# Sparse attention and a channel MLP in one kernel: masks of the later batches written into PSUM by ScalarE, one wide product with U for each batch, and the first scores of a batch two slots later

## The chip, the core and the metric

The kernel runs on one core of one Trainium2 chip. The metric is the device time of one execution in microseconds (us). The engines named below are PE (TensorE, matrix products), DVE (VectorE), ACT (ScalarE), POOL (GpSimd) and SP (SyncE, which issues most DMAs). Each engine carries out its own instructions strictly in the order in which they were written into its stream; engines wait for each other through semaphores.

## The reference

Attention with two kinds of heads, and then a token mixer of low rank and a channel MLP. Heads 0 to 3 see a window of 32 positions (local heads); heads 4 to 7 see positions with the same remainder by 32 (strided heads).

```python
B, H, S, D = 8, 8, 576, 64
scores = q @ k.T / sqrt(D)                      # for each batch and head
mask_local   = (rel >= 0) & (rel < 32)          # heads 0-3, rel = row - column
mask_strided = (rel >= 0) & (same remainder by 32)  # heads 4-7
scores = where(mask, scores, -1e9)
attn = exp(scores - max); attn = attn / (sum(attn) + 1e-9)
x = (attn @ v) as (8, 576, 512)                 # heads side by side
u = x + (x.T @ U @ V).T                         # U: 576x32, V: 32x576
out = u + relu(u @ w_ch1) @ w_ch2               # 512 -> 2048 -> 512
```

## The kernel before

**GEMM stages.** The MLP is done in nine stages, n = 0 to 8, of 512 rows each: stage n is batch n's rows 0 to 511, and stage 8 holds the 64 last rows of all eight batches. A stage has 16 steps, fc = 0 to 15, one for each 128 hidden channels. `gemm1(fc)` makes 12 matmuls of 128x512 into a PSUM tile `ph` (three products for precision, with `uh`, `ul` the high and low part of u, and a high and a low part of the weights). ScalarE takes the relu of it into `gh` (line 652), VectorE makes the low part `gl` (line 653). `gemm2(fc)` makes 12 matmuls from `gh` and `gl` into the two tiles `acc` (line 665); it stands one step behind `gemm1`, so a step is 24 matmuls. At a stage's end `finish` (line 672, four VectorE additions) takes `acc` out, and `split` makes the next stage's `uh` (ScalarE, line 639, four casts) and `ul` (VectorE, line 640, four subtractions) from `raw`.

**Attention between the matmuls.** While stage n runs, batch n+1's attention and mixing are issued in 32 slots, two to a step. `advance(slot)` spreads a fixed number of pieces (the yields of the generator `attention`) evenly between a first and a last slot; `A_EARLY` holds first slot, last slot and number of pieces for stage 0, `A_LATE` for stages 1 to 6. Batches 0 and 1 have their attention before the first stage. For a later batch the order is:

- `local_pairs`: two pairs of local heads. The mask is put into the PSUM tile `px` by two matmuls (line 340), 36 pairs of small score matmuls add to it (line 346), VectorE takes maximum and difference (lines 356, 357), ScalarE the exponential (361), PE transposes (368), ScalarE copies (371), PE multiplies by v (381), VectorE normalises (390 to 397). `px` is a single buffer of two banks.
- `mix_t`, half 0: x^T U for the 256 columns of the local heads (matmuls of lines 514 and 518, then `ta`, lines 523 and 525, and `tst`, lines 527 to 529).
- `strided_copies` (ScalarE, lines 487 and 491), then `mix_t`, half 1, for the columns of the strided heads, `mix_u` (product with V, line 537, and addition, line 539), `mix_tail` (line 546, addition line 552), `transposes` (line 619) and DMAs into `raw`.

**Strided heads.** They use no matmul: `strided_heads` makes products on GpSimd and sums them on VectorE, on a schedule of its own (`S0`, `S1`). Scores come first (GpSimd line 442, VectorE reductions line 444, 27 a batch); the softmax (lines 453 to 461) falls at the boundary of two stages; the second half, with v (GpSimd line 470, VectorE reductions line 472, 27 a batch, whose input grows from 128x64 to 128x576 elements over the first nine), fills the first part of the next stage.

In stage 0, VectorE and ScalarE also convert the last weights from 64-bit words (`weights`, lines 131, 132 and 206).

A scheduler fixes each engine's stream; `tc.issue_after(x)` forces what is issued inside it to stand behind instruction x.

Of the kernel before, what the change touches and what calls it, by code (L numbers as in the profile page):

```python
# [7 lines left out]
F32 = mybir.dt.float32  # L8
F32R = mybir.dt.float32r
# [4 lines left out]
ALU = mybir.AluOpType  # L14
# [1 line left out]
NEG = -1.0e9  # L16
ATT_BUFS = 5
NSP = 2
N_EARLY = 20
N_LATE = 48  # L20
N_STRIDED = 66
LAG = 1
CLA = 4
# [1 line left out]
N_LEAD = 4  # L25
BEHIND = 5
A_EARLY = (5, 28, N_EARLY)
A_LATE = (1, 28, N_LATE)
A_TAIL = (4, 20, 8)
S0 = {2: 16, **{b: 32 * (b - 1) - 12 for b in range(3, 8)}}  # L30
S1 = (14, 14)
# [6 lines left out]
def fused_kernel(ctx, tc, pairs, strided, U, V, w_in, masks, eye, out):  # L38
    nc = tc.nc
    B, S, DM = out.shape  # L40
    D = 64
# [10 lines left out]
    ap_ = ctx.enter_context(tc.tile_pool(name="ap", bufs=1))  # L52
# [28 lines left out]
    marks = {}  # L81
# [24 lines left out]
    mask_l, ident_b = masks_sb[:, 0:320], masks_sb[:, 320:448]  # L106
    U_sb = const.tile([128, 5, R], F32, name="U_sb")
# [8 lines left out]
    raws, w_parts = {}, {}  # L116
# [101 lines left out]
    xgs, tails, tsts, o_str = {}, {}, {}, {}  # L218
    halves = [slice(64 * hh, 64 * hh + 64) for hh in range(2)]
# [109 lines left out]
        for i4 in range(2):  # L329
            far_dma(out=xt[tb + 32 * i4:tb + 32 * i4 + 32, 256:512], in_=ov[16 + i4])  # L330

    def scores(kT, qT, mask):

        sp = psx2()
        done = marks.setdefault("scores", [])
        with tc.issue_after(done[-1]) if len(done) == 1 else nullcontext():
            for n in range(WARM.get(len(done), 0)):
                nc.tensor.matmul(sp[:, 0, :], zeros[:, 0:128], zeros[:, 128:640], start=True, stop=True, skip_group_check=True)
        for hh in range(2):
            nc.tensor.matmul(sp[:, hh, 0:320], ident_b, mask, start=True, stop=False, skip_group_check=True)  # L340
        for c in range(NCH):
            t, c4 = c // 4, c % 4
            k0 = max(0, 32 * c - 32)
            x0 = 64 * t + (0 if c else 32)
            for hh, rows in enumerate(halves):
                last = nc.tensor.matmul(sp[32 * c4:32 * c4 + 32, hh, x0:64 * t + 64], qT[rows, 32 * c:32 * c + 32],  # L346
                                        kT[rows, k0:32 * c + 32], start=False, stop=True, skip_group_check=True,
                                        tile_position=(64 * hh, 32 * c4))
        done.append(last.ins)
        return sp[:, :, 0:320].rearrange("p h (t x) -> p h t x", x=64)  # L350
# [22 lines left out]

    def outputs(PT, vt):

        op = psx2()
        for c in range(NCH):
            t, c4 = c // 4, c % 4
            for o4 in (c4,) if t < 4 else (c4, c4 + 2):
                for hh, rows in enumerate(halves):  # L380
                    last = nc.tensor.matmul(op[32 * o4:32 * o4 + 32, hh, (D + 1) * t:(D + 1) * t + D + 1],  # L381
                                            PT[rows, 32 * c:32 * c + 32], vt[rows, c], start=True, stop=True,
                                            skip_group_check=True, tile_position=(64 * hh, 32 * o4))
        marks.setdefault("PV", []).append(last.ins)
        return op[:, :, 0:5 * (D + 1)].rearrange("p h (t x) -> p h t x", x=D + 1)

# [14 lines left out]
    def local_pairs(b):  # L401

        xg, xt = x_tiles(b)
        tb = 64 * (b % 2)
        for pr in range(2):
            kT, qT = load_qk(b, pr)
            vt = load_v(b, pr)
            for _ in range(2):
                yield
            sp = scores(kT, qT, mask_l)  # L410
            yield
            s_sb = yield from probabilities(sp)
# [83 lines left out]
    def x_tiles(b):  # L496
        if b not in xgs:
            xgs[b] = xp.tile([128, 4, DM], F32, name="xg")
        if b // 2 not in tails:
            tails[b // 2] = xp.tile([128, DM], F32, name="xt")  # L500
        return xgs[b], tails[b // 2]

    def mix_t(b, half):

        xg, xt = x_tiles(b)
        tb = 64 * (b % 2)
        cs = slice(256 * half, 256 * half + 256)
        ps_a = psx1()[:, 0:256]
        if b not in tsts:
            tsts[b] = ap_.tile([96, DM], F32R, name="tst")  # L510
        tst = tsts[b]
        with tc.issue_after(marks["acc"][2 + half]) if b < NSP else nullcontext():
            for j in range(4):
                nc.tensor.matmul(ps_a[32 * j:32 * j + 32, :], U_sb[:, j, :], xg[:, j, cs], start=True, stop=False,  # L514
                                 skip_group_check=True, tile_position=(0, 32 * j))
        for j in range(4):
            part = slice(64 * j, 64 * j + 64)
            nc.tensor.matmul(ps_a[32 * j:32 * j + 32, part], U_sb[tb:tb + 64, 4, :],
                             xt[tb:tb + 64, 256 * half + 64 * j:256 * half + 64 * j + 64], start=False, stop=True,
                             skip_group_check=True, tile_position=(tb, 32 * j))  # L520
        yield
        ta = att([32, 256], "ta")
        nc.scalar.copy(out=ta, in_=ps_a[0:32, :])  # L523
        for j in range(1, 4):
            nc.vector.tensor_tensor(out=ta, in0=ps_a[32 * j:32 * j + 32, :], in1=ta, op=ALU.add)  # L525
        yield
        nc.scalar.copy(out=tst[0:32, cs], in_=ta)
        nc.scalar.copy(out=tst[64:96, cs], in_=ta)
        nc.vector.tensor_tensor(out=tst[32:64, cs], in0=ta, in1=tst[0:32, cs].bitcast(F32), op=ALU.subtract)
        yield  # L530

    def mix_u(b):
# [62 lines left out]
    def attention(b):  # L595
        if b >= NSP:
            yield from local_pairs(b)
            yield from mix_t(b, 0)
            yield "strided"
            yield from strided_copies(b)  # L600
            yield from mix_t(b, 1)
            yield
            yield from mix_u(b)
            yield from mix_tail(b)
            yield from transposes(b)
        else:
            yield from mix_tail(0)
            for half in range(2):
                yield from mix_t(b, half)
            yield from mix_u(b)  # L610
            yield from mix_tail(b)
            yield from transposes(b)
# [31 lines left out]
    def gemm1(fc, dcs=range(NDC)):  # L644
        ph = ps_h.tile([128, 512], F32, name="ph")
        for dc in dcs:
            for i, (part, ut) in enumerate(((0, uh), (0, ul), (1, uh))):
                nc.tensor.matmul(ph, w_parts[fc, 0][:, part, 128 * dc:128 * dc + 128], ut[:, dc, :],  # L648
                                 start=(dc == dcs[0] and i == 0), stop=(dc == dcs[-1] and i == 2))
# [3 lines left out]
        low = nc.vector.scalar_tensor_tensor(out=gl, in0=ph, scalar=0.0, in1=gh.bitcast(F32), op0=ALU.max, op1=ALU.subtract)  # L653
        marks.setdefault("gl", []).append(low.ins)
        return gh, gl
# [172 lines left out]
```

## Time and profile before

| | before |
|---|---|
| median of 3 runs | 930.89 us (1476.99, 928.80, 930.89) |
| profiled execution, its own time | 928.37 us |
| its span in the trace | 926.1 us |
| mean granted TensorE clock | 0.991 |
| PE busy | 902.6 us (97% of the span) |
| DVE busy | 548.6 us (59%) |
| POOL busy | 338.4 us (37%) |
| ACT busy | 244.2 us (26%) |

All durations below are of that one profiled execution. The span is the time from its first to its last instruction; 2.3 us of the execution lie outside it. An engine's busy time counts its arithmetic, not the instructions that only wait or issue DMAs. The granted clock is the share of the full TensorE clock that the chip's throttle allowed. A bracket at the end of a row gives the idle time of the engine ahead of it, and which instruction's end released it.

### The profile page before, as it was taken

To read this page: it belongs to the slowest core of one execution; us is meant where nothing else is said; L and a number is where in the kernel's file an instruction comes from. 1 tells how busy PE (TensorE), PEld (TensorE's weight loads), DVE (VectorE), ACT (ScalarE), POOL (GpSimd) and SP (SyncE) were. 2 spreads that over 40 slices of the span, in tenths; PEclk is the share of its full clock that TensorE was granted. 3 is DMA by queue.
4 is the path that set the end of the run, shared out by engine and by line. 5 is a ranking of instruction groups with operands and counts; after the bars stand their busy time and mean duration, and the time that the engine had idled before them with its cause. 6 is when DMAs were issued, how large, how long until landed. Compare 5 with 4: busy or idle time off the path is not lost.

```text
span 926.1 us, 16819 instructions
## 1 busy us (share of the span) xinstructions
PE 902.6 (97%) x6997; PEld 718.0 (78%) x6998; DVE 548.6 (59%) x895; ACT 244.2 (26%) x478; POOL 338.4 (37%) x378
## 2 busy tenths in 40 slices
PE   7899989999999999999999999999999999999997
PEld 4667767777887788778877787778877888888885
DVE  4579996665886588658765786667863341122111
ACT  3457522142123312331224121422142111121110
POOL 1223493343853393429433764356530000000000
PEclk9899999999999999999999999999999999999999
DMA  9869313201230125011500141014200230001001
GB/s 352 299 205 357 117 54 107 73 2 52 76 145 2 52 55 178 1 52 33 181 8 18 50 168 50 1 53 148 73 1 1 57 120 17 1 1 46 0 1 46
DMA packets 39036, 75.29 MB, mean 81 GB/s; under 512 B 6464, under 2 KB 22864, under 8 KB 37040
## 3 DMA queue, kind: packets, MB, share of 16 engines
q1 hardware_dynamic: 27312, 66.87, 20.7%
q10 hardware_dynamic: 10560, 4.73, 2.0%
q0 software_dynamic: 1088, 2.62, 0.8%
q8 instruction: 55, 0.90, 0.4%
q14 instruction: 21, 0.17, 0.1%
HBM read 54.14 MB, written 11.67 MB: 71 GB/s over the span
## 4 chain that ended last, share of the span: by engine, by line
PE 84%; DVE 4%; DMA 2%; POOL 1%; issue 1%; ACT 0%; SPq 0%; DVEq 0%; ACTq 0%; POOLq 0%
PE acc L665 40%; PE ph L648 39%; PE px L381 1%; DMA w<-in_w_dram 1%; PE px L346 1%; DVE cv L132 1%; DVE s_st L444 1%; PE px L368 1%; PE px L514 1%; DMA od<-x 1%; PE px L537 1%; DMA st<-in_strided_dram 1%; DVE w L206 1%; POOL tmp L442 1%; DVE gl L653 0%
## 5 line engine op out<-in xcount | busy, mean ns | idle before, releaser
L653 DVE SCALAR_TENSOR_TENSOR gl<-ph,gh 128x512 fp32r<-128x512 f32 x144 | 98.9, 688 | 230.1 <-ACT gh L652 229.4
L648 PE MATMUL ph<-uh,w 128*128 128x512 f32 x648 | 215.9, 394 | 0.0
L652 ACT ACTIVATE gh<-ph 128x512 fp32r<-128x512 f32 x144 | 86.2, 599 | 476.9 <-PE ph L648 400.8
L470 POOL TENSOR_TENSOR tmp<-st,s_st 128x448 f32<-128x448 f32 (+7 forms) x162 | 137.3, 876 | 190.8 <-DVE st L472 106.8
L442 POOL TENSOR_TENSOR tmp<-st 128x576 f32<-128x576 f32 (+6 forms) x162 | 175.0, 1121 | 76.5 <-DMA st<-in_strided_dram 66.6
L665 PE MATMUL acc<-w,gh 128*128 128x512 f32 x648 | 196.8, 391 | 0.0
L648 PEld LDWEIGHTS ph<-uh,w 128*128 128x128 f32 x648 | 121.9, 189 | 26.8
L665 PEld LDWEIGHTS acc<-w,gh 128*128 128x128 f32 x648 | 121.3, 188 | 25.6
L472 DVE TENSOR_REDUCE st<-tmp 128x64 f32<-128x64 f32 (+8 forms) x162 | 136.3, 878 | 7.8 <-POOL tmp L470 7.0
L648 PE MATMUL ph<-ul,w 128*128 128x512 f32 x324 | 126.8, 391 | 0.0
L665 PE MATMUL acc<-w,gl 128*128 128x512 f32 x324 | 121.6, 392 | 4.1 <-DVE gl L653 4.1
L444 DVE TENSOR_REDUCE s_st<-tmp 128x9 f32<-128x576 f32 (+6 forms) x162 | 87.2, 563 | 17.5 <-POOL tmp L442 16.7
L665 PEld LDWEIGHTS acc<-w,gl 128*128 128x128 f32 x324 | 61.0, 188 | 18.4 <-DVE gl L653 5.2
L648 PEld LDWEIGHTS ph<-ul,w 128*128 128x128 f32 x324 | 61.1, 189 | 12.6
L487 ACT COPY xg<-st 32x256 f32<-32x256 f32 x96 | 38.8, 404 | 9.1 <-DVE st L472 7.7
L525 DVE TENSOR_TENSOR ta<-px,ta 32x256 f32<-32x256 f32 x42 | 17.6, 420 | 36.5 <-ACT ta L523 35.6
L672 DVE TENSOR_TENSOR xg<-acc,xg 128x512 f32<-128x512 f32 x36 | 22.9, 682 | 13.4 <-PE acc L665 13.4
L539 DVE TENSOR_TENSOR xg<-px,xg 128x512 f32<-128x512 f32 x28 | 18.0, 684 | 11.9 <-PE px L537 11.9
L648 PE MATMUL ph<-uh,w6a 128*128 128x512 f32 x72 | 24.3, 398 | 0.0
L640 DVE TENSOR_TENSOR ul<-raw,uh 128x512 fp32r<-128x512 f32 x32 | 21.1, 682 | 5.3 <-ACT uh L639 5.3
L648 PE MATMUL ph<-uh,w1a 128*128 128x512 f32 x72 | 23.9, 391 | 0.0
L648 PE MATMUL ph<-uh,w2a 128*128 128x512 f32 x72 | 23.9, 391 | 0.0
(265 smaller groups left out, 1252.9 us busy)
## 6 DMA issues: line engine op xcount, KB each, us to landing
w<-in_w_dram SPq DMA_DIRECT2D x9, 1024.0 KB, 13.3
out_dram<-xg SPq DMA_DIRECT2D x32, 256.0 KB, 2.1
v<-in_pairs_dram SPq DMA_DIRECT2D x12, 585.0 KB, 5.1
st<-in_strided_dram SPq DMA_DIRECT2D x6, 1152.0 KB, 5.4
qk<-in_pairs_dram SPq DMA_DIRECT2D x12, 576.0 KB, 5.1
late<-in_pairs_dram SPq DMA_DIRECT2D x8, 585.0 KB, 8.3
late<-in_pairs_dram SPq DMA_DIRECT2D x8, 576.0 KB, 8.1
raw<-bt SPq DMA_DIRECT2D x128, 32.0 KB, 1.9
```

The costliest lines, as they stand in the source:

```text
L442: nc.gpsimd.tensor_tensor(out=tmp[:, 0:n], in0=sk[:, j0:j0 + n], in1=sq[:, i:i + 1].broadcast_to([128, n, D]), op=ALU.mult)
L444: late.append(lambda tmp=tmp, n=n, i=i, j0=j0: nc.vector.tensor_reduce(out=s_st[:, i, j0:j0 + n], in_=tmp[:, 0:n], axis=AX.X, op=ALU.add))
L470: nc.gpsimd.tensor_tensor(out=tv, in0=sv[:, 0:i + 1, d0:d0 + step], in1=s_st[:, i, 0:i + 1].broadcast_to([128, i + 1, step]), op=ALU.mult)
L472: late.append(lambda tv=tv, i=i, d0=d0, step=step: nc.vector.tensor_reduce(out=o_st[:, i, d0:d0 + step], in_=tv.rearrange("p j d -> p d j" ...
L487: nc.scalar.copy(out=xg[32 * i4:32 * i4 + 32, :, cs], in_=o_st[rows, i4:16:4, :])
L539: nc.vector.tensor_tensor(out=xg[:, t + s, :], in0=pv[:, s, :], in1=xg[:, t + s, :], op=ALU.add)
L640: nc.vector.tensor_tensor(out=lo, in0=raw[:, :, :, dc, :], in1=hi.bitcast(F32), op=ALU.subtract)
L648: nc.tensor.matmul(ph, w_parts[fc, 0][:, part, 128 * dc:128 * dc + 128], ut[:, dc, :], start=(dc == dcs[0] and i == 0), stop=(dc == dcs[-1 ...
L652: marks.setdefault("gh", []).append(nc.scalar.activation(out=gh, in_=ph, func=AF.Relu).ins)
L653: low = nc.vector.scalar_tensor_tensor(out=gl, in0=ph, scalar=0.0, in1=gh.bitcast(F32), op0=ALU.max, op1=ALU.subtract)
L665: last = nc.tensor.matmul(accs[n][s // 2][:, s % 2, :], gt[:, cs], w_parts[fc, 1][:, part, :], start=(fc == 0 and i == 0 and n > 0), stop= ...
L672: nc.vector.tensor_tensor(out=ot, in0=accs[n][s // 2][:, s % 2, :], in1=ot, op=ALU.add)
```

## The change

Batches 2 to 7 (the third to the eighth) are changed in these places; batches 0 and 1 keep their masks on PE:

- The mask of a pair of local heads is written into `px` by one ScalarE copy that broadcasts it to both banks (`masked`), a piece of its own ahead of the scores. The scores may be issued only behind the last matmul of the newest `gemm1`.
- In `outputs`, only the matmuls of the first of five column blocks carry `start`; the others are issued behind those. (This holds for all batches.)
- `mix_t` is one group of 512 columns, after the strided copies, for stage 0's batch 1 too.
- `A_LATE` starts at slot 3 and not 1; the numbers of pieces are 47 and 17, and not 48 and 20.

```diff
-A_LATE = (1, 28, N_LATE)          # N_LATE = 48, N_EARLY = 20
+A_LATE = (3, 28, N_LATE)          # N_LATE = 47, N_EARLY = 17
...
+    def masked():
+        sp = psx2()
+        nc.scalar.copy(out=sp[:, :, 0:320], in_=mask_l.broadcast_to([128, 320, 2]).rearrange("p x h -> p h x"))
+        return sp
...
     def outputs(PT, vt):
         op = psx2()
+        first = None
         for c in range(NCH):
             t, c4 = c // 4, c % 4
-            for o4 in (c4,) if t < 4 else (c4, c4 + 2):
-                for hh, rows in enumerate(halves):
-                    last = nc.tensor.matmul(op[...], PT[...], vt[...], start=True, stop=True, ...)
+            with tc.issue_after(first) if t else nullcontext():
+                for o4 in (c4,) if t < 4 else (c4, c4 + 2):
+                    for hh, rows in enumerate(halves):
+                        last = nc.tensor.matmul(op[...], PT[...], vt[...], start=t == 0, stop=True, ...)
+            if t == 0:
+                first = last.ins
...
     def local_pairs(b):
-            sp = scores(kT, qT, mask_l)
+            sp = masked()
+            yield
+            with tc.issue_after(marks["ph"][-1]):
+                sp = scores(kT, qT, mask_l, sp)
...
-    def mix_t(b, half):
-        cs = slice(256 * half, 256 * half + 256)
-        ps_a = psx1()[:, 0:256]
+    def mix_t(b):
+        ps_a = psx1()
         for j in range(4):
-                nc.tensor.matmul(ps_a[32 * j:32 * j + 32, :], U_sb[:, j, :], xg[:, j, cs], ...)
+                nc.tensor.matmul(ps_a[32 * j:32 * j + 32, :], U_sb[:, j, :], xg[:, j, :], ...)
         for j in range(4):
-            part = slice(64 * j, 64 * j + 64)
+            part = slice(128 * j, 128 * j + 128)
...
-        ta = att([32, 256], "ta")
+        ta = att([32, 512], "ta")
...
     def attention(b):
             yield from local_pairs(b)
-            yield from mix_t(b, 0)
             yield "strided"
             yield from strided_copies(b)
-            yield from mix_t(b, 1)
+            yield from mix_t(b)
...
     def gemm1(fc, dcs=range(NDC)):
-                nc.tensor.matmul(ph, w_parts[fc, 0][...], ut[:, dc, :], ...)
+                last = nc.tensor.matmul(ph, w_parts[fc, 0][...], ut[:, dc, :], ...)
+        marks.setdefault("ph", []).append(last.ins)
```

Line numbers grow with the change: 444 becomes 465, 472 becomes 493 (reductions of the strided heads), 552 becomes 569 (addition of the tail), 619 becomes 634 (transposes), 640 becomes 655 (`ul`), 653 becomes 669 (`gl`), 672 becomes 688 (`finish`); on PE, 665 becomes 681 (`gemm2`) and 546 becomes 563 (the tail's product).

The change also moves instructions in the streams of the engines. VectorE at the boundary of stages 3 and 4, from `gl` of the last steps of stage 3 (first row) to `gl` of fc 0 of stage 4 (last row), before:

```order
L653 SCALAR_TENSOR_TENSOR gl<-ph,gh 128x512 x2
L458 TENSOR_REDUCE m_st<-s_st 128x18
L640 TENSOR_TENSOR ul<-raw,uh 128x512
L459 TENSOR_SCALAR m_st<-m_st 128x18
L640 TENSOR_TENSOR ul<-raw,uh 128x512 x2
L460 RECIPROCAL m_st<-m_st 128x18
L640 TENSOR_TENSOR ul<-raw,uh 128x512
L461 TENSOR_TENSOR s_st<-s_st,m_st 128x324
L472 TENSOR_REDUCE st<-tmp 128x64 x5
L672 TENSOR_TENSOR xg<-acc,xg 128x512 x2
L472 TENSOR_REDUCE st<-tmp 128x64
L672 TENSOR_TENSOR xg<-acc,xg 128x512 x2
L653 SCALAR_TENSOR_TENSOR gl<-ph,gh 128x512 x2
```

The same place with the change:

```order
L655 TENSOR_TENSOR ul<-raw,uh 128x512
L481 RECIPROCAL m_st<-m_st 128x18
L655 TENSOR_TENSOR ul<-raw,uh 128x512
L482 TENSOR_TENSOR s_st<-s_st,m_st 128x324
L655 TENSOR_TENSOR ul<-raw,uh 128x512 x2
L493 TENSOR_REDUCE st<-tmp 128x64 x5
L688 TENSOR_TENSOR xg<-acc,xg 128x512 x2
L493 TENSOR_REDUCE st<-tmp 128x64 x2
L688 TENSOR_TENSOR xg<-acc,xg 128x512 x2
L493 TENSOR_REDUCE st<-tmp 128x64 x2
L669 SCALAR_TENSOR_TENSOR gl<-ph,gh 128x512
L493 TENSOR_REDUCE st<-tmp 128x32 x2
```

Six reductions of the strided heads stood ahead of the `gl` of fc 0; now nine do. At the boundary of stages 1 and 2 it is ten, at that of 4 and 5 eleven, and at both the second pair of `finish` stands behind ten of them.

ScalarE at the same boundary, from the last two relus of stage 3, with the change (`s_st` is the exponential of the strided softmax):

```order
L668 ACTIVATE gh<-ph 128x512 x2
L476 ACTIVATE s_st<-s_st 128x324
L343 CAST px<-masks_sb 128x2x320
L654 CAST uh<-raw 128x512 x4
L668 ACTIVATE gh<-ph 128x512 x3
```

The new copy of the mask for the first pair of the next batch (line 343) stands ahead of the four casts of `uh`; before, the casts followed line 455, the same exponential, directly.

VectorE in stage 3 ahead of `gl` of fc 13 (the last row), before; `px` in line 552 is the tail's product:

```order
L444 TENSOR_REDUCE s_st<-tmp 128x6
L552 TENSOR_TENSOR xt<-px,xt 64x512
L444 TENSOR_REDUCE s_st<-tmp 128x9
L444 TENSOR_REDUCE s_st<-tmp 128x7
L653 SCALAR_TENSOR_TENSOR gl<-ph,gh 128x512
```

PE at the tail's product (line 546), before; `w_1500` holds the weights of fc 12, `w_1544` those of fc 13:

```order
L648 MATMUL ph<-uh,w_1544 128x512
L665 MATMUL acc<-w_1500,gh 128x512 x4
L546 MATMUL px<-tst,Vst 64x512
L665 MATMUL acc<-w_1500,gl 128x512
L665 MATMUL acc<-w_1500,gh 128x512 x2
```

With the change VectorE still has two reductions, of widths 7 and 9, between the tail's addition (now line 569) and `gl` (now 669). On PE the tail's product has moved; `w_1531` now holds the weights of fc 13, `w_1572` those of fc 14:

```order
L663 MATMUL ph<-uh,w_1572 128x512
L563 MATMUL px<-tst,Vst 64x512
L681 MATMUL acc<-w_1531,gh 128x512 x4
L681 MATMUL acc<-w_1531,gl 128x512
L681 MATMUL acc<-w_1531,gh 128x512 x2
```

It stood inside `gemm2` of fc 12 and stands 20 matmuls later, directly ahead of `gemm2` of fc 13, whose fifth matmul reads the `gl` of fc 13. So VectorE's addition of the tail, which has to have that product, and the `gl` of fc 13 behind it, now follow a matmul that comes four matmuls ahead of the first user of this `gl`.

Scores of a stage's two pairs stand at 2.5 and 6.0 steps into the stage (before: 1.0 and 4.3), the product with U at 10.0 steps (before: 7.7 and 9.5). At fc 0 of a stage, `gemm2` now has four matmuls with `gh` ahead of the first with `gl` (before: two), and the third writes the second tile of `acc`.

More of the change, by code (lines that the diff above doesn't have):

```diff
@@ L18 @@
 NSP = 2
-N_EARLY = 20
-N_LATE = 48
+N_EARLY = 17
+N_LATE = 47
 N_STRIDED = 66
@@ L330, in od_reads, with with_mask @@
             far_dma(out=xt[tb + 32 * i4:tb + 32 * i4 + 32, 256:512], in_=ov[16 + i4])
-    def scores(kT, qT, mask):
-        sp = psx2()
+    def with_mask(sp, mask):
         done = marks.setdefault("scores", [])
@@ L340, in scores @@
             nc.tensor.matmul(sp[:, hh, 0:320], ident_b, mask, start=True, stop=False, skip_group_check=True)
+    def masked():
+        sp = psx2()
+        nc.scalar.copy(out=sp[:, :, 0:320], in_=mask_l.broadcast_to([128, 320, 2]).rearrange("p x h -> p h x"))
+        return sp
+    def scores(kT, qT, mask, sp=None):
+        if sp is None:
+            sp = psx2()
+            with_mask(sp, mask)
+        done = marks.setdefault("scores", [])
         for c in range(NCH):
@@ L376, in outputs @@
         op = psx2()
+        first = None
         for c in range(NCH):
             t, c4 = c // 4, c % 4
-            for o4 in (c4,) if t < 4 else (c4, c4 + 2):
-                for hh, rows in enumerate(halves):
-                    last = nc.tensor.matmul(op[32 * o4:32 * o4 + 32, hh, (D + 1) * t:(D + 1) * t + D + 1],
-                                            PT[rows, 32 * c:32 * c + 32], vt[rows, c], start=True, stop=True,
-                                            skip_group_check=True, tile_position=(64 * hh, 32 * o4))
+            with tc.issue_after(first) if t else nullcontext():
+                for o4 in (c4,) if t < 4 else (c4, c4 + 2):
+                    for hh, rows in enumerate(halves):
+                        last = nc.tensor.matmul(op[32 * o4:32 * o4 + 32, hh, (D + 1) * t:(D + 1) * t + D + 1],
+                                                PT[rows, 32 * c:32 * c + 32], vt[rows, c], start=t == 0, stop=True,
+                                                skip_group_check=True, tile_position=(64 * hh, 32 * o4))
+            if t == 0:
+                first = last.ins
         marks.setdefault("PV", []).append(last.ins)
@@ L501, in x_tiles @@
         return xgs[b], tails[b // 2]
-    def mix_t(b, half):
+    def mix_t(b):
         xg, xt = x_tiles(b)
         tb = 64 * (b % 2)
-        cs = slice(256 * half, 256 * half + 256)
-        ps_a = psx1()[:, 0:256]
[L509 to L512, printed above, removed]
+        ps_a = psx1()
+        tst = tsts[b] = ap_.tile([96, DM], F32R, name="tst")
+        with tc.issue_after(marks["acc"][3]) if b < NSP else nullcontext():
             for j in range(4):
-                nc.tensor.matmul(ps_a[32 * j:32 * j + 32, :], U_sb[:, j, :], xg[:, j, cs], start=True, stop=False,
+                nc.tensor.matmul(ps_a[32 * j:32 * j + 32, :], U_sb[:, j, :], xg[:, j, :], start=True, stop=False,
                                  skip_group_check=True, tile_position=(0, 32 * j))
         for j in range(4):
-            part = slice(64 * j, 64 * j + 64)
-            nc.tensor.matmul(ps_a[32 * j:32 * j + 32, part], U_sb[tb:tb + 64, 4, :],
-                             xt[tb:tb + 64, 256 * half + 64 * j:256 * half + 64 * j + 64], start=False, stop=True,
-                             skip_group_check=True, tile_position=(tb, 32 * j))
+            part = slice(128 * j, 128 * j + 128)
+            nc.tensor.matmul(ps_a[32 * j:32 * j + 32, part], U_sb[tb:tb + 64, 4, :], xt[tb:tb + 64, part],
+                             start=False, stop=True, skip_group_check=True, tile_position=(tb, 32 * j))
         yield
-        ta = att([32, 256], "ta")
+        ta = att([32, 512], "ta")
         nc.scalar.copy(out=ta, in_=ps_a[0:32, :])
@@ L526, in mix_t @@
         yield
-        nc.scalar.copy(out=tst[0:32, cs], in_=ta)
-        nc.scalar.copy(out=tst[64:96, cs], in_=ta)
-        nc.vector.tensor_tensor(out=tst[32:64, cs], in0=ta, in1=tst[0:32, cs].bitcast(F32), op=ALU.subtract)
+        nc.scalar.copy(out=tst[0:32], in_=ta)
+        nc.scalar.copy(out=tst[64:96], in_=ta)
+        nc.vector.tensor_tensor(out=tst[32:64], in0=ta, in1=tst[0:32].bitcast(F32), op=ALU.subtract)
         yield
@@ L607, in attention @@
             yield from mix_tail(0)
-            for half in range(2):
-                yield from mix_t(b, half)
+            yield from mix_t(b)
             yield from mix_u(b)
@@ L647, in gemm1 @@
             for i, (part, ut) in enumerate(((0, uh), (0, ul), (1, uh))):
-                nc.tensor.matmul(ph, w_parts[fc, 0][:, part, 128 * dc:128 * dc + 128], ut[:, dc, :],
-                                 start=(dc == dcs[0] and i == 0), stop=(dc == dcs[-1] and i == 2))
+                last = nc.tensor.matmul(ph, w_parts[fc, 0][:, part, 128 * dc:128 * dc + 128], ut[:, dc, :],
+                                        start=(dc == dcs[0] and i == 0), stop=(dc == dcs[-1] and i == 2))
+        marks.setdefault("ph", []).append(last.ins)
         gh = mp.tile([128, 512], F32R, name="gh", bufs=2)
```

## Prediction

> **What bounds the kernel now.** The page's chain of the work that ended last comes first, then the table of stretches, cut at the stages.
>
> ```profile
> PE 84%; DVE 4%; DMA 2%; POOL 1%; issue 1%; ACT 0%; SPq 0%; DVEq 0%; ACTq 0%; POOLq 0%
> ...
> 362.90:460.30 97.40, 97.40 (x743) 77.77 (x740) 68.08 (x114) 25.45 (x55) 51.03 (x55) 1.00 0.20 64
> ...
> 365.90 2.72 PE ph L648 x12
> ```
>
> The chain is PE's. In stage 3 (the second row: length, busy time of PE, weight loads, DVE, ACT and POOL, then the clock) PE has no idle time in 97.4 us. Twelve GEMM matmuls take 2.72 us, 0.227 each; 16 steps of 24 make 87.0 us, and the other 10.4 are attention's small matmuls. DVE has 68 us of work, so it bounds nothing by its sum, but its order does as soon as something PE needs stands late in it. So I count what PE loses in matmuls, then ask of each `gl`, the only thing that PE needs from DVE in every step, whether it still comes in time.
>
> **The change: what goes.** The masks first, from PE's timeline around the first and the second scores of stage 3's start (first piece) and 21 us later:
>
> ```profile
> 361.71 0.39 PE L648 MATMUL ph<-uh,w1a 128*128 128x512 f32 x1
> 362.03 0.92 PE L346 MATMUL px<-qk 64*32 64x32 f32 x72
> 362.88 0.73 PE L665 MATMUL acc<-w0b,gh 128*128 128x512 f32 x2
> ...
> 382.77 0.39 PE L665 MATMUL acc<-w3b,gh 128*128 128x512 f32 x1
> 383.00 0.45 PE L340 MATMUL px<-masks_sb 128*128 128x320 bf16 x2
> 383.38 0.92 PE L346 MATMUL px<-qk 64*32 64x32 f32 x72
> 384.23 0.50 PE L665 MATMUL acc<-w3b,gh 128*128 128x512 f32 x1
> ...
> 404.80 0.39 PE L648 MATMUL ph<-ul,w 128*128 128x512 f32 x1
> 405.11 0.64 PE L514 MATMUL px<-xg,U_sb 128*32 128x256 f32 x8
> 405.68 0.32 PE L518 MATMUL px<-xt,U_sb 64*32 64x64 f32 x8
> 405.93 0.50 PE L648 MATMUL ph<-uh,w 128*128 128x512 f32 x1
> ```
>
> Scores alone cost 362.88 - 361.71 - 0.23 = 0.94; with masks 384.23 - 382.77 - 0.23 = 1.23. So a mask pair costs 0.29, and 11 of the 12 pairs save 3.2 (the first one, below, stands in an idle time). Half a product with U costs 405.93 - 404.80 - 0.23 = 0.90, two 1.80. For one group of twice the width the trace has no row; it costs between 1.0 (a matmul's length does not grow) and 1.8 (it doubles). I take 1.44, since 0.90 is mostly a fixed part: a saving of 0.36, times 6 batches 2.2 (0 to 4.8). Batch 2's scores, scattered in five pieces over stages 0 and 1 now, become one group; each piece costs some 0.1 extra to enter and leave: 0.5.
>
> Stage 0 is bound by DVE until 139 us, and there the order changes:
>
> ```profile
> 130.39 0.50 PE L665 MATMUL acc<-w,gl 128*128 128x512 f32 x1 [1.90 <-DVE gl L653]
> ...
> 137.59 0.45 PE L340 MATMUL px<-masks_sb 128*128 128x320 bf16 x2
> 139.35 0.50 PE L665 MATMUL acc<-w,gl 128*128 128x512 f32 x1 [1.32 <-DVE gl L653]
> ...
> 136.13 2.45 DVE L132 SCALAR_TENSOR_TENSOR cv<-w,cv 128x1024 int32<-128x1024 int32 x1
> ...
> 140.33 1.29 DVE L619 STREAM_TRANSPOSE bt<-xg 128x512 f32<-128x512 f32 x2
> ...
> 130.00:132.00 2.00, 1.61 (x7) 1.31 (x8) 2.00 (x4) 0.71 (x2) 2.00 (x2) 0.96 0.12 33
> 132.00:134.00 2.00, 2.00 (x6) 1.58 (x5) 1.94 (x4) 0.00 (x0) 2.00 (x3) 0.50 0.00 0
> 134.00:136.00 2.00, 2.00 (x8) 1.56 (x7) 2.00 (x2) 0.00 (x0) 2.00 (x3) 0.69 0.35 131
> ```
>
> The conversion of 2.45 us falls behind the `gl` that ends the wait at 139.35, and transposes of 1.29 come ahead of it: 1.2 earlier, and the 1.32 goes. The 1.90 wait may go too, and with it the half clock behind it (the three stretches, column before last but two): 2 x (0.04 + 0.50 + 0.31) = 1.7 us lost. I take 2.0 off, of 0 to 4.9. All gains: 3.2 + 2.2 + 0.5 + 2.0 = **7.9**.
>
> **What is added on ScalarE.** Twelve copies of 128x640; the nearest row is the exponential of that size:
>
> ```profile
> L361 ACT ACTIVATE s_sb<-s_sb 128x640 f32<-128x640 f32 x12 | 8.9, 741 | 39.3 <-DVE s_sb L357 39.3
> ...
> 449.45 2.17 ACT L639 CAST uh<-raw 128x512 fp32r<-128x512 f32 x4
> ```
>
> That is 0.7 each, and ScalarE has 72 us to spare in a stage, so they cost nothing, save six that stand ahead of the casts of `uh` and make `ul` about 0.5 later (next). Wider copies of `ta` and `tst` lie in the same cover. DMA order on SP is unchanged.
>
> **First new wait: `gl` of fc 0.** DVE and PE at the boundary of stages 3 and 4, before:
>
> ```profile
> 453.77 0.65 DVE L472 TENSOR_REDUCE st<-tmp 128x64 f32<-128x64 f32 x2 [0.46 <-POOL tmp L470]
> 454.60 0.38 DVE L472 TENSOR_REDUCE st<-tmp 128x64 f32<-128x192 f32 x1 [0.17 <-POOL tmp L470]
> 455.17 1.42 DVE L472 TENSOR_REDUCE st<-tmp 128x64 f32<-128x256 f32 x2 [0.19 <-POOL tmp L470]
> ...
> 459.65 1.28 DVE L653 SCALAR_TENSOR_TENSOR gl<-ph,gh 128x512 fp32r<-128x512 f32 x2
> ...
> 462.44 3.08 DVE L472 TENSOR_REDUCE st<-tmp 128x64 f32<-128x448 f32 x3
> ...
> 460.22 0.73 PE L665 MATMUL acc<-w0b,gh 128*128 128x512 f32 x2
> 460.78 0.39 PE L665 MATMUL acc<-w0b,gl 128*128 128x512 f32 x1
> ```
>
> Today `gl` starts at 459.65 and is read at 460.78: no slack worth the name. With the change the three reductions of 462.44 (3.0 in the queue) stand ahead of it. Add 0.5 for the later `uh`, take off 0.8 for the idle times in the first three rows, which the earlier softmax closes: start 462.35, end 463.0. PE, without the scores ahead (0.94) and with four matmuls ahead of the first `gl`, wants it at 460.22 - 0.94 + 4 x 0.227 = 460.2. Wait **2.8** at the boundaries 2-3, 3-4 and 5-6. One reduction more at 1-2 makes 3.4, two at 4-5 make 4.1 (0.7 each; there the second tile of `acc` also comes free late). Sum 8.4 + 3.4 + 4.1 = **15.9**. At 0-1 and 6-7 no strided work of that kind is ahead of it.
>
> **Second new wait: `gl` of fc 13.** PE's tail product and DVE behind it, before:
>
> ```profile
> 437.82 0.40 PE L546 MATMUL px<-tst,Vst 96*64 96x512 f32 x1
> ...
> 438.26 0.68 DVE L552 TENSOR_TENSOR xt<-px,xt 64x512 f32<-64x512 f32 x1
> 438.87 1.42 DVE L444 TENSOR_REDUCE s_st<-tmp 128x9 f32<-128x576 f32 x2
> 440.20 0.68 DVE L653 SCALAR_TENSOR_TENSOR gl<-ph,gh 128x512 fp32r<-128x512 f32 x1
> ...
> 443.86 0.39 PE L665 MATMUL acc<-w,gl 128*128 128x512 f32 x1
> ```
>
> The `gl` ends at 440.88, 3.06 after the tail's product starts, and has three microseconds of slack before 443.86. With the change the same queue stands behind a product that is 0.23 + 4 x 0.227 = 1.14 ahead of the reader: wait 1.92, in stages 1 to 5, which have strided scores there: **9.6**.
>
> **The clock.** The half clock followed a wait of 1.90; none followed the one of 1.32. Waits of 2.8 and more lie above both; I let four of five cost 1.7, and half of the five at 1.9: 6.8 + 4.2 = **11.0**, bounds 0 and 17. The Trainium skill, "TensorE: Matmul & The Clock Gate", section "HAM oscillation — how this bites in real kernels", names idle times over about 3.4 us as what drops the clock; the trace disagrees, with its drop behind 1.90. By that rule only the waits of 3.4 and 4.1 would drop, and the sum would be 949.5.
>
> **Sum,** against the profiled execution's own 928.4 (the median of the runs shown, 930.9, is 0.3% above it): 928.4 - 7.9 + 15.9 + 9.6 + 11.0 = **957**.
>
> **Rivals.**
>
> - *The clock holds through these waits*, or through all but the longest, as it held through 1.32: 946 to 950. For it speaks that only one drop is in the trace; against, that it came behind less. The skill's rule, above, is of this kind.
> - *Only the boundary waits.* DVE reaches the tail with time in hand, or the scheduler's reductions there cost less than 3.06: 957 - 9.6 - 4.2 = 943. Against it: the queue behind the tail's addition is the same by kind.
> - *Faster: both waits are covered.* If DVE reached `gl` of fc 0 2.8 earlier and that of fc 13 1.9 earlier, only gains are left: 928.4 - 7.9 = 920.5. DVE's idle times ahead of `gl` at the boundary add up to 0.8, too little.
> - *The mask copy blocks ScalarE.* It needs the single `px`, which the last pair's normalisation must leave first; `gh` queues behind it. Each of 6 second copies could cost 1 to 2: 963 to 969. All ten waits dropping the clock gives 963 too.
> - *The change doesn't do what it says:* were the masked copy as dear in PE's time as the masks, 3.2 of the gains would go: 960, inside the forecast.
>
> **How the numbers follow.** Forecast (951 to 962) 0.60; clock holds 0.15; only boundary waits 0.12; covered 0.05; blocked ScalarE or all drops 0.08. The range 940 to 966 leaves out the covered case and about half of the last. Within 2% (what a measurement of this kernel can tell from no change; up to about 947 to 949) are the boundary case and half of the holding clock: 0.20. Faster by over 2% needs more than the gains seen: 0.02. Slower: 0.78.
>
> **What would show it.** PE waits on DVE's `gl` (line 669), about ten, of 1.9 and of 2.8 to 4.1, at fc 0 and fc 13; dips of the clock behind them; stages 1 to 5 of 101 to 104 in place of 97.3, stages 6 to 8 slightly shorter; masked copy 0.7, product with U about 1.4. I am wrong if PE stays without idle time in stages 1 to 5, or if the waits are there on ScalarE's `gh`.

## The result and the profile after

The changed kernel takes 954.47 us (median of 4 runs, 953.85 to 956.49) against 929.85 for the kernel before: a ratio of 1.0274, 95% interval 1.0248 to 1.0301. Here and below the ratio leaves out slow runs, of which the kernel before had one, of 1476.99. The changed kernel is slower, 2.5 us below the 957 that was forecast. The profiled execution took 954.44, its span is 952.6.

In the chain of the work that ended last PE has gone from 84% to 73%, and DVE, DMA and POOL have taken its place:

```profile
PE 73%; DVE 10%; DMA 7%; POOL 4%; issue 2%; SPq 1%; ACT 1%; DVEq 0%; POOLq 0%; ACTq 0%
```

The table of stretches of the changed kernel, cut where `gemm2` of fc 1 starts in each stage (length, busy time of PE, weight loads, DVE, ACT, POOL, clock, DMA):

```profile
0.00:168.60 168.60, 152.43 (x1829) 115.32 (x1830) 130.77 (x209) 71.64 (x113) 69.51 (x88) 0.97 0.59 211
168.60:273.40 104.80, 99.52 (x720) 79.10 (x719) 68.57 (x111) 26.22 (x54) 53.48 (x57) 0.97 0.19 61
273.40:376.60 103.20, 98.43 (x720) 78.37 (x719) 67.65 (x109) 26.33 (x54) 52.04 (x55) 0.98 0.20 64
376.60:481.00 104.40, 99.99 (x720) 79.12 (x719) 67.20 (x109) 26.33 (x54) 51.94 (x55) 0.97 0.19 61
481.00:585.30 104.30, 98.42 (x720) 78.02 (x719) 67.84 (x109) 26.30 (x54) 51.91 (x55) 0.98 0.19 64
585.30:686.70 101.40, 96.93 (x721) 77.15 (x721) 67.08 (x109) 26.33 (x54) 52.02 (x55) 1.00 0.19 63
686.70:782.90 96.20, 96.20 (x721) 77.32 (x720) 46.22 (x67) 25.45 (x52) 12.82 (x13) 1.00 0.14 42
```

The same table of the kernel before, its first two stretches:

```profile
0.00:173.80 173.80, 156.75 (x1917) 117.45 (x1919) 128.91 (x212) 72.37 (x116) 65.70 (x84) 0.96 0.58 208
173.80:271.20 97.40, 97.40 (x741) 77.73 (x741) 70.57 (x116) 25.41 (x55) 53.11 (x58) 1.00 0.20 65
```

The first stretch is 5.2 shorter. Each of the next five, 97.3 or 97.4 before, is 4.1 to 7.4 longer, 31.5 in all; what follows is the same within 0.3. DVE's busy time in a stage has hardly changed, and PE has idle time where it had none.

PE's timeline of the changed kernel, the waits from stage 1 on (in brackets the idle time and its releaser; line 669 is `gl`, line 688 `finish`):

```profile
245.71 0.51 PE L681 MATMUL acc<-w,gl 128*128 128x512 f32 x1 [1.62 <-DVE gl L669]
265.54 1.22 PE L681 MATMUL acc<-w0b,gh 128*128 128x512 f32 x2 [3.66 <-DVE xg L688]
350.86 0.50 PE L681 MATMUL acc<-w,gl 128*128 128x512 f32 x1 [1.90 <-DVE gl L669]
370.38 0.78 PE L681 MATMUL acc<-w0b,gl 128*128 128x512 f32 x1 [2.87 <-DVE gl L669]
453.81 0.50 PE L681 MATMUL acc<-w,gl 128*128 128x512 f32 x1 [1.63 <-DVE gl L669]
470.88 0.73 PE L681 MATMUL acc<-w0b,gh 128*128 128x512 f32 x2 [0.90 <-DVE xg L688]
473.48 0.80 PE L681 MATMUL acc<-w0b,gl 128*128 128x512 f32 x1 [1.87 <-DVE gl L669]
558.43 0.50 PE L681 MATMUL acc<-w,gl 128*128 128x512 f32 x1 [1.90 <-DVE gl L669]
578.25 0.90 PE L681 MATMUL acc<-w0b,gh 128*128 128x512 f32 x2 [3.66 <-DVE xg L688]
579.47 0.79 PE L681 MATMUL acc<-w0b,gl 128*128 128x512 f32 x1 [0.33 <-DVE gl L669]
662.50 0.50 PE L681 MATMUL acc<-w,gl 128*128 128x512 f32 x1 [1.62 <-DVE gl L669]
681.96 0.50 PE L681 MATMUL acc<-w0b,gl 128*128 128x512 f32 x1 [2.85 <-DVE gl L669]
```

Two places in each of five stages: fc 13 (`w,gl`, 1.62 to 1.90, 8.7 in all) and fc 0 (`w0b`, at the boundaries 3.66, 2.87, 2.77, 3.99 and 2.85, 16.1 in all). The clock at the five boundaries, in stretches of 20 us:

```profile
262.00:282.00 20.00, 16.46 (x128) 13.12 (x129) 10.77 (x16) 2.01 (x4) 5.07 (x7) 0.83 0.20 66
367.00:387.00 20.00, 17.13 (x136) 13.52 (x135) 11.92 (x16) 2.18 (x4) 5.46 (x7) 0.91 0.14 45
469.00:489.00 20.00, 17.23 (x130) 13.14 (x129) 11.16 (x16) 2.53 (x4) 5.58 (x8) 0.83 0.21 69
574.00:594.00 20.00, 16.02 (x131) 12.22 (x130) 11.57 (x17) 2.54 (x4) 5.83 (x8) 0.91 0.22 79
679.00:699.00 20.00, 17.16 (x144) 13.73 (x144) 11.54 (x16) 2.58 (x4) 5.60 (x8) 1.00 0.12 38
```

20 x (0.17 + 0.09 + 0.17 + 0.09) = 10.4 lost to half clock, at four boundaries of five; the clock has two decimals only, so 10.2 would do as well.

DVE at the boundary 3-4 shows the new order (five, two and two reductions of line 493 ahead of `gl`) in time:

```profile
463.95 0.21 DVE L493 TENSOR_REDUCE st<-tmp 128x64 f32<-128x64 f32 x1
...
466.70 1.28 DVE L688 TENSOR_TENSOR xg<-acc,xg 128x512 f32<-128x512 f32 x2
467.89 1.74 DVE L493 TENSOR_REDUCE st<-tmp 128x64 f32<-128x384 f32 x2
469.55 1.28 DVE L688 TENSOR_TENSOR xg<-acc,xg 128x512 f32<-128x512 f32 x2
470.74 2.09 DVE L493 TENSOR_REDUCE st<-tmp 128x64 f32<-128x512 f32 x2
472.74 0.69 DVE L669 SCALAR_TENSOR_TENSOR gl<-ph,gh 128x512 fp32r<-128x512 f32 x1
```

From 466.70 to 472.74 DVE has no pause: the second pair of `finish` (PE waits for it until 470.88) and `gl` (until 473.48) stand behind reductions that nobody waits for yet.

The other place, DVE ahead of `gl` of fc 13 in stage 3; the tail's product starts on PE at 450.83:

```profile
451.27 0.68 DVE L569 TENSOR_TENSOR xt<-px,xt 64x512 f32<-64x512 f32 x1 [0.61 <-PE px L563]
451.88 1.28 DVE L465 TENSOR_REDUCE s_st<-tmp 128x7 f32<-128x448 f32 x2
453.07 0.68 DVE L669 SCALAR_TENSOR_TENSOR gl<-ph,gh 128x512 fp32r<-128x512 f32 x1
```

In all five stages DVE stands idle for 0.61 to 0.65 there, until the tail's product is done.

The gains are there as well: the wide product with U costs 427.92 - 426.25 - 0.23 = 1.44 on PE, the figure that the prediction took:

```profile
426.25 0.39 PE L663 MATMUL ph<-uh,w 128*128 128x512 f32 x1
426.57 1.06 PE L532 MATMUL px<-xg,U_sb 128*32 128x512 f32 x8
427.56 0.42 PE L536 MATMUL px<-xt,U_sb 64*32 64x128 f32 x8
427.92 0.50 PE L681 MATMUL acc<-w,gh 128*128 128x512 f32 x1
```

### The profile page after: what moved, and what is told of

Same layout as the page of the kernel before. It is cut to its first block, busy times and chain, and to the rows that moved or that the text cites. A ratio compares the mean times of both kernels' runs of the same rounds, so it can differ in the third digit from the quotient of the medians.

```text
span 952.6 us, 16505 instructions
## 1 busy us (share of the span) xinstructions
PE 905.3 (95%) x6862; PEld 719.3 (76%) x6862; DVE 544.8 (57%) x867; ACT 248.9 (26%) x469; POOL 343.7 (36%) x378
## 4 chain that ended last, share of the span: by engine, by line
PE 73%; DVE 10%; DMA 7%; POOL 4%; issue 2%; SPq 1%; ACT 1%; DVEq 0%; POOLq 0%; ACTq 0%
PE acc L681 34%; PE ph L663 33%; DVE st L493 3%; DMA st<-in_strided_dram 2%; POOL tmp L463 2%; POOL tmp L491 2%; DVE xg L688 2%; PE px L397 1%; DMA qk<-in_pairs_dram 1%; DMA w0a<-in_w_dram 1%; DMA w<-in_w_dram 1%; SPq L96 1%; PE px L357 1%; DVE s_st L465 1%; PE px L379 1%
## 5 line engine op out<-in xcount | busy, mean ns | idle before, releaser
L663 PE MATMUL ph<-uh,w 128*128 128x512 f32 x648 | 213.2, 389 | 0.0
L463 POOL TENSOR_TENSOR tmp<-st 128x576 f32<-128x576 f32 (+6 forms) x162 | 177.5, 1131 | 92.5 <-DVE s_st L465 52.2
L491 POOL TENSOR_TENSOR tmp<-st,s_st 128x448 f32<-128x448 f32 (+7 forms) x162 | 141.8, 903 | 186.2 <-DVE st L493 128.3
L681 PE MATMUL acc<-w0b,gh 128*128 128x512 f32 x72 | 26.2, 456 | 8.6 <-DVE xg L688 8.6
L655 DVE TENSOR_TENSOR ul<-raw,uh 128x512 fp32r<-128x512 f32 x32 | 23.2, 746 | 5.2 <-ACT uh L654 3.7
L681 PEld LDWEIGHTS acc<-w0b,gh 128*128 128x128 f32 x72 | 15.6, 223 | 13.6 <-DVE xg L688 10.3
L663 PE MATMUL ph<-uh,w5a 128*128 128x512 f32 x72 | 24.5, 401 | 0.0
L681 PE MATMUL acc<-w0b,gl 128*128 128x512 f32 x36 | 17.0, 507 | 7.9 <-DVE gl L669 7.9
```

The costliest lines, as they stand in the source:

```text
L463: nc.gpsimd.tensor_tensor(out=tmp[:, 0:n], in0=sk[:, j0:j0 + n], in1=sq[:, i:i + 1].broadcast_to([128, n, D]), op=ALU.mult)
L491: nc.gpsimd.tensor_tensor(out=tv, in0=sv[:, 0:i + 1, d0:d0 + step], in1=s_st[:, i, 0:i + 1].broadcast_to([128, i + 1, step]), op=ALU.mult)
L655: nc.vector.tensor_tensor(out=lo, in0=raw[:, :, :, dc, :], in1=hi.bitcast(F32), op=ALU.subtract)
L663: last = nc.tensor.matmul(ph, w_parts[fc, 0][:, part, 128 * dc:128 * dc + 128], ut[:, dc, :], start=(dc == dcs[0] and i == 0), stop=(dc == ...
L681: last = nc.tensor.matmul(accs[n][s // 2][:, s % 2, :], gt[:, cs], w_parts[fc, 1][:, part, :], start=(fc == 0 and i == 0 and n > 0), stop= ...
```

## The experiments

Theory A is the prediction's: the order on DVE makes both `gl` late. Rival B puts it on the new copy on ScalarE, or on the wide product with U.

**The later first slot alone, and the change without it.**

```diff
-A_LATE = (1, 28, N_LATE)
+A_LATE = (3, 28, N_LATE)      # in the kernel before: e1_start_only; the reverse in the changed kernel: e2_change_start1
```

> The kernel before with one edit: the first slot of A_LATE 3 and not 1. Theory A (the later slot alone brings more strided reductions ahead of the gl of fc 0, nine or ten by the order): PE waits of 2.8 to 4.1 at five boundaries, with dips of the clock behind most, 940 to 955; the tail's product is 2.95 ahead of its reader, so at most 0.4 a stage for the gl of fc 13. Rival B (ScalarE's mask copy ahead of uh, or the wide product with U, is what makes gl late): no new waits, 925 to 931.

> The whole change but A_LATE's first slot 1 as before. Theory A: six reductions ahead of the gl of fc 0 again, the tail's product 13.5 steps into the stage, so both waits go and the gains stay: 917 to 923. Rival B: the waits stay, 945 to 955. In between (930 to 940) if only one of the two waits goes.

e1 took 941.38, 1.0152 (1.0134 to 1.0170) of before, without any mask copy; e2 took 921.04, 0.9932 (0.9912 to 0.9952), with all of them. So the first slot in `A_LATE` decides whether the change is slow, and rival B falls as the cause by itself. In e1 PE waits at all five boundaries, but only 0.5 to 1.5 us each, not 2.8 to 4.1. Its timeline at 3-4:

```profile
468.81 0.31 PE L346 MATMUL px<-qk 64*32 64x64 f32 x6
469.82 0.73 PE L665 MATMUL acc<-w0b,gh 128*128 128x512 f32 x2 [0.70 <-DVE xg L672]
```

Two things differ from the whole change there. Some of the first scores stand between the matmuls of fc 0 and fill part of the time, and `uh` isn't held up by a mask copy. The size of the waits is therefore the shift's together with the other parts: put into the kernel before, the later slot costs 13 us; taken out of the change, it gives 33 back. What the copy adds by making `uh` later (0.6: in the change it stands at 459.54 on ScalarE and the casts at 460.16) no run takes out alone. Nor are e1's 13 us the predicted mechanism only: in its profile stages 1 to 5 are 14.2 longer than before, of which PE is idle for 5.5, half clock takes 1.7, and the other 7 are PE working longer, with the first scores of a stage in three or four pieces. In e2 the boundary waits and those of fc 13 are gone.

**The tail's product earlier.**

```diff
+        marks["tail"] = nc.tensor.matmul(pv[0:tb + 64], Vst[...], tsts[b], ...).ins
...
+                with tc.issue_after(marks["tail"]) if fc == 14 and dc == dcs[0] and i == 0 else nullcontext():
                     last = nc.tensor.matmul(ph, w_parts[fc, 0][...], ut[:, dc, :], ...)
```

> The changed kernel, with the first matmul of gemm1 of fc 14 put behind the tail's product, which so comes half a step (2.72) earlier. Theory A (the gl of fc 13 is late because the tail's product comes late): the five waits of 1.6 to 1.9 go, 945 to 947. Rival C (VectorE's queue between the gl of fc 12 and that of fc 13 is too long by itself, and the tail's product holds it up by 0.6 only): the waits shrink to 1.0 to 1.3, 951 to 952.

It took 953.19, 1.0284 (1.0259 to 1.0309): nothing gained. The five waits are still 1.53 to 1.75. DVE in stage 2 of this kernel:

```profile
345.51 0.69 DVE L569 TENSOR_TENSOR xt<-px,xt 64x512 f32<-64x512 f32 x1
346.24 1.74 DVE L465 TENSOR_REDUCE s_st<-tmp 128x6 f32<-128x384 f32 x3
348.57 0.76 DVE L465 TENSOR_REDUCE s_st<-tmp 128x9 f32<-128x576 f32 x1 [0.59 <-POOL tmp L463]
349.36 0.69 DVE L670 SCALAR_TENSOR_TENSOR gl<-ph,gh 128x512 fp32r<-128x512 f32 x1
```

The tail's addition now comes without delay, but four reductions and not two follow it, the last of which waits for GpSimd, and `gl` stays nearly where it was. So the late product is not what the waits hang on. That leaves the queue, rival C, but even the 0.6 that DVE had waited for the tail didn't come back: in its place comes the wait for GpSimd, 0.59 in these rows.

**The queue ahead of `gl` of fc 13 earlier.**

```diff
-A_LATE = (3, 28, N_LATE)
+A_LATE = (3, 27, N_LATE)
```

> The changed kernel with A_LATE's last slot 27 and not 28, which brings the product with V and the tail half a step earlier and so takes a pair of additions out of VectorE's queue between the gl of fc 12 and that of fc 13; nine to eleven reductions stay ahead of the gl of fc 0. Theory C (that queue is what makes the gl of fc 13 late): its five waits go (8.7 in all), the boundary waits stay: 944 to 947. Theory A in its first form (the late tail's product alone): as well, since the tail comes 0.46 steps earlier too; but the experiment before spoke against it. If neither: 951 to 955.

It took 944.22, 1.0183 (1.0160 to 1.0206): no wait of fc 13 is left in its trace, and those of fc 0 are (3.40, 3.65, 3.92, 2.64 and 2.91). The profiles differ by 9.1 in their spans (943.5 for 952.6), the 8.7 of these waits and little else. The edit doesn't do to the queue what was expected: the same pair of additions with V still stands between `gl` of fc 12 and of fc 13 in every stage, and nine strided reductions are left of eleven. What it does is to put the products with V and the tail's product about half a step earlier on PE (2.5 us in stage 2), so that all of this queue runs earlier. Taken with e3, in which the tail's product alone came earlier, this points to the whole queue from the product with V on, and not to its last item; how much of it is DVE's own work and how much GpSimd's pace, no run takes apart.

**The reductions behind `gl` of fc 0.**

```diff
+                def reduce(...):
+                    first = marks["gl"][NFC * (b - 1):NFC * (b - 1) + 1]
+                    with tc.issue_after(first[0]) if i >= 5 and first else nullcontext():
                         nc.vector.tensor_reduce(out=o_st[:, i, d0:d0 + step], ...)
```

> The changed kernel, with the strided reductions of the second half from the sixth on put behind the gl of fc 0 of their stage: five stand ahead of it. Theory A: the boundary waits (16.1) and the half clock behind them (10.2) go, 926 to 931. Rival D (the pushed-back reductions come late for something else, gl of fc 1 or the first scores' maximum): part comes back, 933 to 945.

It took 929.48, 1.0012 (0.9997 to 1.0028), inside 926 to 931. No boundary wait is in its trace, and the five of fc 13 are as in the change. Pushing the reductions back costs nothing that shows.

**Both mended** (last slot 27; `i >= 4`).

> The changed kernel with A_LATE's last slot 27, and the strided reductions of the second half from the fifth on put behind the gl of fc 0. Theory: both waits and the half clock behind them go and all the gains stay: 918 to 922, as with the first slot 1. If the later scores cost something by themselves: 923 to 930.

It took 917.45, 0.9889 (0.9868 to 0.9909): the lowest median of the study, below the kernel before and the changed one. Its stage 2 in the table of stretches:

```profile
265.10:361.30 96.20, 96.20 (x720) 77.33 (x719) 68.22 (x110) 26.32 (x54) 51.90 (x56) 1.00 0.21 69
```

PE is busy throughout, and the stage takes 1.1 less than the 97.3 of before. The later scores cost nothing by themselves: in e2, with the first slot 1, a stage takes 97.0, as the first scores come out in pieces there.

**PE kept busy while it waits.**

```diff
+    zb = const.tile([128, 128], BF16, name="zb")
+    nc.vector.memset(zb, 0.0)
...
+                if fc == 0 and 2 <= n <= 6 and s == 0 and i == 1:
+                    with tc.issue_after(last.ins):
+                        for _ in range(14):
+                            marks["fill"] = nc.tensor.matmul(accs[n][0][:, 0, 0:448], zb, masks_sb, start=False, stop=False).ins
...
```

> The changed kernel with 14 matmuls of 128x448 with zeros (2.6 us) added to gemm2 of fc 0 at the boundaries 1-2 to 5-6, behind its first two matmuls: PE works while it waits, and the sums are unchanged. If the clock drops because PE stands idle there: the idle times shrink to 0.3 to 1.3, no half clock at the boundaries, 10.2 less: 943 to 946. If it drops for another reason: the half clock stays and 954 to 958.

The weights `zb` are zeros, so the sums stay as they are. It took 946.20, 1.0199 (1.0175 to 1.0222), 8.3 less than the change, for 13 us more matmuls. PE's timeline at the boundary 2-3:

```profile
363.79 2.82 PE L690 MATMUL acc<-masks_sb,zb 128*128 128x448 bf16 x14
366.29 0.79 PE L685 MATMUL acc<-w0b,gh 128*128 128x512 f32 x2
367.31 0.50 PE L685 MATMUL acc<-w0b,gl 128*128 128x512 f32 x1 [0.23 <-DVE gl L671]
```

No half clock is left at the five boundaries; one came behind the wait of 1.90 at fc 13 of stage 4. The data waited for came no sooner, so this is the price of the clock by itself: 10.4 less the 1.7 of that new drop would be 8.7.

**The same kernels once more.**

> The changed kernel as it is, profiled once more. In its first profile the half clock starts and ends at whole multiples of 3.41 us from one another, and its boundary 5-6 had a wait of 2.85 without one. Theory G (the clock is set by how much of a window of 3.41 us, on a fixed grid, PE stood idle; about 1.9 to 2.0 of it): the waits come out the same within 0.1, their places on the grid differ, and so other boundaries drop or none; ahead of each drop lies a window with 1.9 or more idle, and a long wait that the grid cuts into parts below that drops nothing. Rival H (the length of the wait, or what runs behind it, decides): the same four boundaries drop as in the first profile, for the same lengths.

> The kernel with the last slot 27, profiled once more. In its first profile the wait of 3.65 at 2-3 dropped nothing, while four others of 2.6 to 3.9 did. Theory G: the waits are the same, and the boundary without a drop is another one or none, by the grid. Rival H: 2-3 is again the one without a drop.

The waits came out the same within 0.1 in both. In the second profile of the change half clock came behind all five boundaries and behind two waits of 1.90, and it took 958.6. Behind `gl` of fc 13 in stage 2 (a wait of 1.90 until 350.86 in the first profile, and of 1.90 until 350.39 in the second) the table of stretches has, first and then second profile, the clock third from the end:

```profile
350.80:354.20 3.40, 3.35 (x14) 2.74 (x15) 2.31 (x5) 0.60 (x1) 2.37 (x2) 1.00 0.29 65
```

```profile
350.80:354.20 3.40, 3.40 (x11) 2.70 (x10) 2.30 (x5) 0.15 (x1) 1.88 (x2) 0.59 0.26 59
```

The kernel with last slot 27 waits 3.65 at the boundary 2-3, in PE's timeline and in the stretch behind it; first profile:

```profile
366.66 0.73 PE L681 MATMUL acc<-w0b,gh 128*128 128x512 f32 x2 [3.65 <-DVE xg L688]
```

```profile
367.80:371.20 3.40, 3.40 (x16) 2.81 (x15) 0.64 (x2) 0.00 (x0) 0.84 (x1) 1.00 0.16 56
```

Second profile:

```profile
366.40 0.73 PE L681 MATMUL acc<-w0b,gh 128*128 128x512 f32 x2 [3.65 <-DVE xg L688]
```

```profile
367.80:371.20 3.40, 3.40 (x10) 2.66 (x9) 0.38 (x1) 0.00 (x0) 0.70 (x1) 0.55 0.07 25
```

The same wait dropped the clock once and once not, so rival H falls. In each trace, drops begin and end at whole multiples of 3.41 us from one another, and behind these waits they last 3.4 or 6.8. Laid on that grid, with cells of 3.41 us, the wait of 3.65 that dropped nothing is cut into 1.94 and 1.71, and idle times of 1.57 to 1.78 in one cell dropped nothing, while 1.90 in one cell did in the kernel before, in e4 and in e7. The edge isn't sharp: at 5-6 in the change's first profile 1.93 in a cell dropped nothing, and in e1 a cell with 1.54 idle and some small score matmuls did. That PE's share of work in a cell decides fits nearly all; what counts as work in it stays open.

**Parts alone.** e8 puts only the masks into the kernel before (with `outputs` and `issue_after` as in the change):

```diff
-            sp = scores(kT, qT, mask_l)
+            sp = masked()
+            yield
+            with tc.issue_after(marks["ph"][-1]):
+                sp = scores(kT, qT, mask_l, sp)
```

e11 puts only the wide product with U into it:

```diff
             yield from local_pairs(b)
-            yield from mix_t(b, 0)
             yield "strided"
             yield from strided_copies(b)
-            yield from mix_t(b, 1)
+            yield from mix_t(b)
```

e12 is the mended kernel with the masks of batches 2 to 7 on PE again:

```diff
-            sp = masked()
             yield
             with tc.issue_after(marks["ph"][-1]):
-                sp = scores(kT, qT, mask_l, sp)
+                sp = scores(kT, qT, mask_l)
```

> The kernel before with the masks of batches 2 to 7 put into PSUM by ScalarE, and with no other part of the change (two products with U, first slot 1, pieces 50 and 22): six reductions ahead of the gl of fc 0, by the order. Theory A: no boundary waits; masks save 3.2, the first scores of a stage, which come out in pieces, give 1 to 3 back: 925 to 928. Rival B (the copy ahead of uh makes gl late): 940 to 955.

> The kernel before with one product with U of 512 columns for each batch and no other part of the change (pieces 45 and 17, masks on PE, first slot 1): 6 x 0.36 = 2.2 less, and 0 to 2 from stage 0: 924 to 926. If the later product brings waits of its own: 928 or more.

> The kernel of the experiment in which both waits are mended, with the masks of batches 2 to 7 on PE again (two matmuls, one piece less of code between them and the scores). By the order no wait comes back, so the difference is the masks alone: 12 x 0.29 = 3.5 slower than 917.5, so 920 to 922. If the masks are worth nothing on PE: 917 to 918.

e8 took 928.77, 1.0012 (0.9996 to 1.0027): no gain. No boundary wait is in it, against rival B, but its stage 0 has longer waits (1.45, 2.15 and 1.73, before 0.90, 1.90 and 1.32), one of 1.85 follows in stage 1, and the first scores of a stage come out in two or three pieces. At the boundary 3-4 the mask copy stands ahead of the casts of `uh` as in the change.

e11 took 921.31, 0.9916 (0.9894 to 0.9937), better than the 924 to 926 expected. A stage takes 96.8, 0.5 less than before. But its profiled execution is also 4.4 ahead when the first `gemm2` of fc 1 starts, where its stream on PE has not yet differed; the stretch from 20 to 40 us shows most of the reason (the clock is the third figure from the end), in the kernel before and then in e11:

```profile
20.00:40.00 20.00, 16.19 (x366) 12.41 (x366) 12.07 (x24) 10.14 (x21) 5.89 (x13) 0.83 0.87 311
```

```profile
20.00:40.00 20.00, 16.43 (x458) 12.60 (x458) 14.41 (x28) 12.17 (x26) 5.58 (x14) 1.00 0.94 333
```

The clock ahead of stage 0 differs from execution to execution: that first `gemm2` of fc 1 starts between 68.4 and 73.7 in the profiles of this study. Part of e11's lead in the medians may be that; how much, its five runs don't settle.

e12 took 919.61, 0.9900 (0.9877 to 0.9924). Its interval overlaps e6's, so the runs don't show what the masks are worth. The profiles do, by stages without any wait: 96.8 to 96.9 in e12, 96.2 to 96.3 in e6 (96.7 in stage 5, where the first scores come out in two pieces). Stage 2 of e12:

```profile
266.60:363.40 96.80, 96.80 (x724) 77.50 (x723) 67.71 (x110) 24.97 (x52) 50.68 (x56) 1.00 0.21 69
```

That is 0.6 for two pairs, the 2 x 0.29 of the prediction, 3.5 for all twelve.

## Why the prediction was right

By its own terms, in the profiled execution:

- *Gains of 7.9:* the stretch up to stage 1 is 5.2 shorter, stage 6 is 0.3 longer, and five stages without a wait would be 1.06 shorter each (e6): 5.2 + 5.3 - 0.3 = 10.2. Masks (0.29 a pair, by e12) and the product (1.44) were exact; for the product that is luck, since the reason given ("0.90 is mostly a fixed part") doesn't yield it: by 0.90 and 1.44 only 0.36 is fixed. Stage 0 was under-sized, though within its bounds: the drop behind 1.90 went, and batch 2's scores left it. But its waits only fell from 4.1 to 3.5, and the one of 1.32, which was to go, is still 1.12.
- *`gl` of fc 0, 15.9:* 16.1. The mechanism is shown by e4 (taking the reductions away takes the waits away), and the size at each boundary was met within 0.3. At three of the five boundaries PE waited first for the second tile of `acc`, which the prediction had only at 4-5 as a remark; it lies in the same queue and doesn't change the sum.
- *`gl` of fc 13, 9.6:* 8.7. The size was nearly right, and the rows look as forecast: DVE waits for the tail's product, and `gl` ends 2.92 behind its start (3.06 forecast). The step that failed is to make "a product that is 0.23 + 4 x 0.227 = 1.14 ahead of the reader" the cause: with the product 2.7 earlier (e3) the waits shrank by 0.06 to 0.15 only. DVE's queue from the `gl` of fc 12 on, with its reductions fed by GpSimd, ends no sooner by itself; the tail's addition is one item of it. That both limits fell so close together made the number come out, and that is luck.
- *Clock, 11.0:* 10.4 in this profile. Four of the five boundary waits did drop it, but none of those at fc 13, and some drops lasted 6.8 and not 3.4 us. So that 10.4 lies near 11.0 is luck: the second profile of the same kernel had seven places and lost 13.7. That the length of a wait decides, as the term has it, was too simple. The Trainium skill's rule ("TensorE: Matmul & The Clock Gate", section "HAM oscillation — how this bites in real kernels"), idle times over about 3.4 us, is as far off: 1.90 dropped the clock, and 3.65 once did not. (By that rule the prediction's own terms, 946.0 and two drops of 1.7, give 949.4 and not 949.5.)
- *Not in the sum:* stages 1 to 5 together are 31.5 longer, and 24.8 + 10.4 - 5.3 = 29.9. The other 1.6 is probably time around the waits: a first matmul after one takes 0.50 and not 0.39, which makes 1.3 for twelve.

The rival "faster: both waits are covered" was the change's own potential: 920.5 was its price, and e2 and e6 came to 921.0 and 917.5 once the order was mended. No wait of PE on ScalarE's `gh` is in the trace, so the copy blocked nothing.

## What to carry to other kernels

When a change is scored by what it removes from the busy engine, look at what it does to the order on the engine that delivers to it: here 10 us were gained on PE and 37 lost, 10 of them to half clock, because work that nobody waits for yet stood ahead of the one small result that PE needs in each step. Put such results ahead by an explicit order, and the removed work shows as time. A slot number that only moves the start of a stream of work can decide more than the arithmetic it moves.

## What the runs showed of the hardware

Behind the waits, the half clock came in pieces of 3.4 or 6.8 us on a grid of 3.41 us whose place differs from run to run, so equal waits cost 1.7, 3.4 or nothing, and equal executions of the changed kernel lost 10.4 and 13.7 us to it. Fourteen matmuls with zeros in each waiting time, 2.8 us of work for nothing, made the kernel 8.3 us faster.
